# A transformer block with adaptive layer norm: row maxima split ahead of their transposition, V in 58 columns, two passes moved from VectorE to ScalarE

## The chip, the core and the metric

One core of a Trainium2 chip. It has TensorE (PE, with its weight loads PEld beside the matmuls), VectorE (DVE), ScalarE (ACT), GpSimd (POOL) and SyncE (SP), which here issues the DMAs. Each works through its own instructions in order; semaphores tie them together. The metric is the device time in microseconds, as the median of several runs.

## The reference

```python
mod = (_silu(c) @ w_mod).reshape(c.shape[0], 6, 1, -1)
sa, ca, ga, sb, cb, gb = (mod[:, 0], ..., mod[:, 5])
h = _layernorm(x, axis=-1) * (1 + ca) + sa
x = x + ga * _A_ref(h, A_wqkv, A_wo)      # attention, 16 heads of 28
h = _layernorm(x, axis=-1) * (1 + cb) + sb
x = x + gb * _B_ref(h, B_w1, B_b1, B_w2)  # dense 448 -> 1792, Mish, dense -> 448
...
scores = jnp.einsum("bhqd,bhkd->bhqk", q, k) * (Dh ** -0.5)
mask = (idx[:, None] - idx[None, :] >= 0) & (idx[:, None] - idx[None, :] < W)   # W = 256
scores = jnp.where(mask[None, None], scores, -1e9)
p = _softmax(scores, axis=-1)
o = jnp.einsum("bhqk,bhkd->bhqd", p, v)
```

2048 rows of 448 float32 numbers, one batch.

## The kernel before, in words

Nearly all matmuls run in fp32r, a float32 form that the matmul takes with fewer bits. An operand that needs more is split into a high part (rounded to fp32r by ACT or DVE) and a low part (the difference, by DVE or POOL), and the product is made as high x high + high x low + low x high. Names that end in h or hi and in l or lo are such parts: hh and hl of the normalised input, hho and hlo of the attention's output, Ph and Pl of the probabilities.

The 2048 rows are four groups of 512 (g = 0 to 3). Per group and head there is a slot (64 slots, s), and each slot has three units (192 units, u; k is the unit in the slot). In a unit, the main loop writes, in this order: the delayed stages that are due (pipe.step), the products of the low probabilities with V of three units ago (PV, tile pv), scores and mask for this unit (B, tile sB, then two exponentials P and Ph on ACT), the low part Pl = P - Ph of the last unit on POOL (SP, L768), a first pass over the scores of a slot three ahead for its row maxima (A: matmul sA, then a masked maximum on DVE into a column of mx, L713), in every sixth unit M2, and then fill. M2 serves a pair of slots: PE transposes their eight columns of maxima (tile mt, L719), DVE splits the result into two fp32r rows (mr, L721 and L722), and two DMAs put them into rows 84 and 85 of the query tiles, so that the score matmul subtracts the maximum. What the program writes first, an engine does first.

Fill is work of other groups: qkv products of the next group, then of the group just done the transposition of the attention output (gen_oT, tile ot, four chunks), the product with wo (gen_wo), and for the group after the next the transposed normalised input (gen_hT, tile tr, four chunks ci = 0 to 3). These are generators; each unit adds RATE[g] to a credit, and every piece drawn takes its cost from it:

```python
    RATE = {0: 0.56, 1: 0.87, 2: 0.87, 3: 0.65}
    def step(g):
        return next(fillers[g], 99.0) or RATE[g]
```

So a bare yield costs one unit. A second set of generators (side_step) hands out DVE and ACT work: the modulation's weighted sums (wm), layer norm (xin), weight splits. pipe.add(hold, f1, f2, ...) puts f1, f2, ... into the units that follow. The list later holds DMAs.

For a chunk of gen_hT, PE makes four transposes into a bank of PSUM tagged mm (of two). ACT writes hh from it (hT_hi, L257), a step later DVE makes the unrounded value in place (hT_y, L254) and subtracts hh from it into hl (L262). Then the bank is free. The attention output leaves pv as 60 rows per head (28 high, a row of ones for the sum and three of zeros, 28 low), two heads at partitions 0 and 64 of a tile o; four transposes (et) turn a pair, and ACT, DVE and POOL add the halves and divide (E2, E3).

After the attention (404 us), the MLP runs.

## Time and profile before

| | |
|---|---|
| median of 3 runs | 699.99 us (699.79 to 700.13) |
| the profiled execution | 699.71 us, span 698.0 us |
| granted TensorE clock | 1.000 |
| PE busy | 679.1 us, 97% of the span |
| DVE, ACT, POOL busy | 382.2, 391.7, 334.0 us |

The span runs from the first to the last instruction; the 1.7 us beside it lie around them. Busy time counts an engine's instructions without branches and waits. Since matmuls are pipelined, their records overlap, and an engine that is 97% busy may still lose a little between them.

### The profile page before, as it was taken

The numbers are of one execution on the slowest core, as the hardware profiler recorded it, in microseconds if no ns is written. First come the engines' busy times: TensorE is split into PE (matmuls) and PEld (weight loads), VectorE is DVE, ScalarE is ACT, GpSimd is POOL, SyncE is SP. The second block draws the span as 40 slices with busy tenths as digits, with TensorE's granted clock in tenths as the row PEclk, the third lists the DMA queues.
The fourth block names the chain that finished last, engine by engine and source line by source line (L and its number), as shares of the span: only waits on it lengthen the run. The fifth ranks groups of instructions, "written<-read, shape, count | busy, mean of one in ns | idle before, by whom it ended". The sixth has DMA issues, their size and how long they took to land.

```text
span 698.0 us, 11835 instructions
## 1 busy us (share of the span) xinstructions
PE 679.1 (97%) x3905; PEld 583.6 (84%) x3905; DVE 382.2 (55%) x1030; ACT 391.7 (56%) x741; POOL 334.0 (48%) x372
## 2 busy tenths in 40 slices
PE   8899999999999999999999899999999999999997
PEld 8777788888888888888887688888888888888886
DVE  5688657688665887655768754553125212521112
ACT  4638788777667867667878874353224222422221
POOL 7846779686766776666779967222010000000000
PEclk9999999999999999999999999999999999999999
DMA  7865665365662462763773165810250035001001
GB/s 213 263 226 198 217 213 176 119 201 164 179 206 85 156 211 89 191 211 108 226 217 112 53 211 173 212 29 4 103 120 1 2 105 121 0 2 53 0 1 53
DMA packets 75568, 91.13 MB, mean 131 GB/s; under 512 B 31632, under 2 KB 51838, under 8 KB 75508
## 3 DMA queue, kind: packets, MB, share of 16 engines
q1 hardware_dynamic: 75044, 90.38, 42.5%
q8 instruction: 31, 0.51, 0.3%
q14 instruction: 29, 0.24, 0.1%
q10 hardware_dynamic: 464, 0.00, 0.0%
HBM read 56.60 MB, written 32.51 MB: 128 GB/s over the span
## 4 chain that ended last, share of the span: by engine, by line
PE 82%; DVE 6%; DMA 4%; issue 2%; ACT 2%; POOL 1%; SPq 1%; POOLq 0%; DVEq 0%; ACTq 0%
PE z L950 21%; PE pv L778 9%; PE qk L315 7%; PE acc L1142 7%; PE acc L1140 6%; PE acc L1141 6%; PE sA L711 5%; PE wo L315 5%; PE sB L742 4%; PE qk_v L315 4%; DMA scr<-st 2%; DVE junk L713 2%; PE et L792 2%; PE warm L428 1%; PE sB L753 1%
## 5 line engine op out<-in xcount | busy, mean ns | idle before, releaser
L768 POOL TENSOR_TENSOR Pl<-P,Ph 128x512 fp32r<-128x512 f32 (+2 forms) x192 | 235.0, 1232 | 77.5 <-ACT Ph L761 44.9
L713 DVE CUSTOM_DVE_ANT_0 junk<-sA,mask 128x384 f32<-128x384 f32 (+2 forms) x256 | 135.0, 527 | 91.9 <-PE sA L711 84.5
L760 ACT ACTIVATE P<-sB 128x512 f32<-128x512 f32 (+2 forms) x192 | 109.6, 571 | 58.8 <-PE sB L757 33.7
L958 DVE TENSOR_TENSOR al<-t,ah 128x512 fp32r<-128x512 f32 x56 | 39.2, 699 | 188.6 <-ACT ah L957 188.6
L956 ACT ACTIVATE t<-z,b1c 128x512 f32<-128x512 f32 x56 | 38.4, 686 | 142.9 <-PE z L950 142.6
L761 ACT ACTIVATE Ph<-sB 128x512 fp32r<-128x512 f32 (+2 forms) x192 | 109.0, 568 | 0.0
L711 PE MATMUL sA<-k,q 84*128 84x384 f32 (+2 forms) x256 | 100.7, 396 | 2.6 <-DVE mx L713 1.8
L950 PE MATMUL z<-hlf,w 128*128 128x512 f32 x224 | 88.5, 395 | 0.0
L950 PE MATMUL z<-hhf,w 128*128 128x512 f32 x224 | 88.5, 395 | 0.0
L1140 PE MATMUL acc<-w2h,ah 128*128 128x448 f32 x224 | 82.0, 366 | 0.0
L1142 PE MATMUL acc<-w2h,al 128*128 128x448 f32 x224 | 81.9, 366 | 0.0
L1141 PE MATMUL acc<-w2l,ah 128*128 128x448 f32 x224 | 81.5, 364 | 0.0
L778 PE MATMUL pv<-Ph,v 128*60 128x256 f32 (+2 forms) x352 | 76.7, 292 | 0.6 <-ACT o L784 0.3
L778 PE MATMUL pv<-Pl,v 128*60 128x256 f32 (+2 forms) x352 | 73.8, 283 | 2.9 <-POOL Pl L768 2.0
L742 PE MATMUL sB<-q,k 128*128 128x256 f32 (+1 forms) x352 | 73.7, 283 | 0.6 <-DMA q<-mr 0.6
L950 PE MATMUL z<-hhf,w1l 128*128 128x512 f32 x168 | 66.3, 394 | 0.0
L742 PEld LDWEIGHTS sB<-q,k 128*128 128x128 f32 (+1 forms) x352 | 61.2, 188 | 2.0 <-DMA q<-mr 1.0
L778 PEld LDWEIGHTS pv<-Ph,v 128*60 128x60 f32 x352 | 45.7, 133 | 14.1 <-ACT o L784 1.9
L711 PEld LDWEIGHTS sA<-k,q 84*128 84x128 f32 x256 | 49.6, 195 | 8.0 <-DVE mx L713 5.3
L778 PEld LDWEIGHTS pv<-Pl,v 128*60 128x60 f32 x352 | 45.1, 132 | 11.9 <-POOL Pl L768 4.0
L950 PEld LDWEIGHTS z<-hlf,w 128*128 128x128 f32 x224 | 42.1, 188 | 10.1
L224 POOL COPY xn<-xn 128x64 f32<-128x64 f32 x12 | 4.5, 396 | 93.7 <-DVE xn L241 93.6
(167 smaller groups left out, 1305.0 us busy)
## 6 DMA issues: line engine op xcount, KB each, us to landing
scr<-st SPq DMA_DIRECT2D x24, 512.0 KB
k<-scr SPq DMA_DIRECT2D x48, 252.0 KB
q<-scr SPq DMA_DIRECT2D x64, 168.0 KB
scr<-st SPq DMA_DIRECT2D x32, 256.0 KB
x<-x1d SPq DMA_DIRECT2D x10, 448.0 KB
xin<-in_A_x_dram SPq DMA_DIRECT2D x8, 448.0 KB
xr<-in_A_x_dram SPq DMA_DIRECT2D x16, 224.0 KB
x1d<-xr SPq DMA_DIRECT2D x16, 224.0 KB
```

The costliest lines, as they stand in the source:

```text
L315: PE.matmul(p, b, a, start=(n == 0), stop=(n == 10))
L711: PE.matmul(p[:, c0:384], q[0:84, t * 128:(t + 1) * 128], k[0:84, t * 128 + c0:t * 128 + 384], start=True, stop=True)
L713: DVE.tensor_tensor_reduce(out=junk[:, c0:384], in0=p[:, c0:384], in1=mask[:, c0:384], scale=1.0, scalar=-3.0e38, op0=ALU.add, op1=ALU.max ...
L742: PE.matmul(p[:, c:c + 128 * (t1 - t0)], k[0:rows, jj * 128:(jj + 1) * 128], q[0:rows, t0 * 128:t1 * 128], start=(n == 0), stop=False, ski ...
L760: ACT.activation(P[:, c0:], p[:, c0:], AF.Exp, scale=SCALE)
L761: ACT.activation(Ph[u][:, c0:], p[:, c0:], AF.Exp, scale=SCALE)
L768: eng.tensor_tensor(Pl[u][:, a:b], Pt[u][:, a:b], Ph[u][:, a:b].bitcast(F32), op=ALU.subtract)
L778: PE.matmul(pv[0:60, t0 * 128:t1 * 128], V[j % NV][:, h, :], P[u][:, c:c + 128 * (t1 - t0)], start=(P is Ph and b == 0 and n == 0), stop=F ...
L950: PE.matmul(zb[n], ps[m][1], ps[m][0], start=(m == 0), stop=(m == 10))
L1140: PE.matmul(p, ah[n][:, ts], w2h[f], start=(f == 0), stop=False)
L1141: PE.matmul(p, ah[n][:, ts], w2l[f], start=False, stop=False)
L1142: PE.matmul(p, al[n][:, ts], w2h[f], start=False, stop=(f == NF - 1))
```

## The change

It has four parts.

1. A new M2a, written at the head of the unit that has M2 (ahead of pipe.step), splits the maxima before they are transposed: a cast of the 128x8 columns to fp32r and a subtraction, both from SBUF to SBUF on DVE, into ml, 128x16. M2 then makes one fp32r product of ml with an fp32r identity (ident1, cast once at the start), which gives 16 rows; DVE copies them with one cast, and the two DMAs read rows 0 to 7 and 8 to 15.
2. V has 58 columns a head instead of 60: one row of zeros instead of three. pv, o and et shrink to 58 and 122.
3. hT_two: for chunks 2 and 3 of groups 1 to 3, ACT makes the unrounded value in place right after hh; DVE keeps only the subtraction.
4. gen_oT: after the first chunk of groups 0 to 2 the piece costs 1.2 instead of one unit's rate, so the second chunk and the fill behind it are drawn later.

```diff
+    ident1 = kq.tile([128, 128], F32R, name="ident1")
+    DVE.tensor_copy(ident1, ident)
...
-    V = [(vp if j < 6 else vq).tile([128, H, 60], F32R, name=f"v{j}") for j in range(NV)]
+    V = [(vp if j < 6 else vq).tile([128, H, 58], F32R, name=f"v{j}") for j in range(NV)]
...
+    def hT_two(p, ci, hh):
+        hT_hi(p, ci, hh, 0)
+        if ci > 1:
+            ACT.activation(p, p, AF.Identity, scale=cols[:, 1, ci:ci + 1], bias=cols[:, 0, ci:ci + 1])
...
-            pipe.add(2, lambda p=p, ci=ci: hT_hi(p, ci, hh, 0), lambda p=p, ci=ci: hT_lo(p, ci, hh, hl, 0))
+            pipe.add(2, lambda p=p, ci=ci: hT_two(p, ci, hh), lambda p=p, ci=ci: hT_lo(p, ci, hh, hl, 0, ci < 2))
...
-            yield
+            yield 1.2 if ci == 0 and g < NG - 1 else None
             if g == NG - 1:
...
+    def M2a(pr):
+        ml[pr] = att.tile([128, 2, 8], F32R, name=f"ml{pr}", tag="ml", bufs=2)
+        m = mx[pr].rearrange("p a t -> p (a t)")
+        DVE.tensor_copy(ml[pr][:, 0], m)
+        DVE.tensor_tensor(ml[pr][:, 1], m, ml[pr][:, 0].bitcast(F32), op=ALU.subtract)
...
     def M2(pr):
         p = bank("tr", 1, f"mt{pr}")
-        PE.transpose(p[0:8, 0:128], mx[pr].rearrange("p a t -> p (a t)"), ident)
-        r = att.tile([8, 2, 128], F32R, name=f"mr{pr}", tag="mr", bufs=1)
-        DVE.tensor_copy(r[:, 0], p[0:8, 0:128])
-        DVE.tensor_tensor(r[:, 1], p[0:8, 0:128], r[:, 0].bitcast(F32), op=ALU.subtract)
+        PE.matmul(p[0:16, 0:128], ml[pr].rearrange("p i n -> p (i n)"), ident1, start=True, stop=True)
+        r = att.tile([16, 128], F32R, name=f"mr{pr}", tag="mr", bufs=1)
+        DVE.tensor_copy(r, p[0:16, 0:128])
...
-            PE.matmul(pv[0:60, t0 * 128:t1 * 128], V[j % NV][:, h, :], P[u][:, c:c + 128 * (t1 - t0)],
+            PE.matmul(pv[0:58, t0 * 128:t1 * 128], V[j % NV][:, h, :], P[u][:, c:c + 128 * (t1 - t0)],
...
-            PE.transpose(p[:, t * 128:t * 128 + 124], O2[pr % 2][0:124, t * 128:(t + 1) * 128], ident[0:124, 0:124])
+            PE.transpose(p[:, t * 128:t * 128 + 122], O2[pr % 2][0:122, t * 128:(t + 1) * 128], ident[0:122, 0:122])
...
+        turn = k == 0 and (a - 1) % 2 == 1 and LEAD <= a - 1 < NS
+        if turn:
+            M2a((a - 1) // 2)
         pipe.step()
...
-        if k == 0 and (a - 1) % 2 == 1 and LEAD <= a - 1 < NS:
+        if turn:
             M2((a - 1) // 2)
```

What stands in a row now. First VectorE around the transpose at 370.6 us (the unit with M2 for the 30th pair). Before, the maximum of sA_3, then that of the next pair's sA_0, then the two rows of mr:

```order
799 L713 ISA junk,mx_5426<-sA_3_5573,mask 128x384
800 L713 ISA mx_5426 128x1
801 L713 ISA junk,mx_5597<-sA_0_5598,mask 128x384
802 L713 ISA mx_5597 128x1
803 L721 CAST mr_5603<-mt_5601 8x128
804 L722 TENSOR_TENSOR mr_5603<-mt_5601,mr_5603 8x128
805 L198 TENSOR_TENSOR w1l<-w1p_5289,w_5226 128x448
```

After:

```order
822 L720 ISA junk,mx_5482<-sA_3_5628,mask 128x384
823 L720 ISA mx_5482 128x1
824 L727 CAST ml_5640<-mx_5482 128x8
825 L728 TENSOR_TENSOR ml_5640<-mx_5482,ml_5640 128x8
826 L720 ISA junk,mx_5656<-sA_0_5657,mask 128x384
827 L720 ISA mx_5656 128x1
828 L736 CAST mr_5662<-mt_5660 16x128
829 L200 TENSOR_TENSOR w1l<-w1p_5320,w_5282 128x448
```

The split has moved from behind mt to ahead of it, between the last maximum and mt.

Second, TensorE at the second chunk of the attention output of group 0 (140 to 142 us; sA_3 is the last score pass of the pair, mt its transpose). Before, one ot chunk ahead of pv and one behind mt:

```order
789 L711 MATMUL sA_3_2165<-k_3_148,q_1_460 128x384
790 L250 MATMUL ot_2168<-ident,on_996 128x128 x4
791 L778 MATMUL pv_2174<-Ph_2088,v_167 60x128
792 L778 MATMUL pv_2174<-Ph_2088,v_169 60x384
793 L778 MATMUL pv_2174<-Pl_2125,v_167 60x128
794 L778 MATMUL pv_2174<-Pl_2125,v_169 60x384
795 L742 MATMUL sB_2180<-q_0_377,k_1_144 128x384
796 L742 MATMUL sB_2180<-q_0_377,k_1_144 128x128
797 L753 LDWEIGHTS identr
798 L753 MATMUL sB_2180<-fdmask,identr 128x2x128
799 L711 MATMUL sA_0_2191<-k_4_150,q_2_461 128x384
800 L719 MATMUL mt_2194<-ident,mx_1999 8x128
```

After:

```order
789 L718 MATMUL sA_3_2187<-k_3_148,q_1_462 128x384
790 L792 MATMUL pv_2190<-Ph_2110,v_169 58x128
791 L792 MATMUL pv_2190<-Ph_2110,v_171 58x384
792 L792 MATMUL pv_2190<-Pl_2147,v_169 58x128
793 L792 MATMUL pv_2190<-Pl_2147,v_171 58x384
794 L756 MATMUL sB_2198<-q_0_379,k_1_144 128x384
795 L756 MATMUL sB_2198<-q_0_379,k_1_144 128x128
796 L767 LDWEIGHTS identr
797 L767 MATMUL sB_2198<-fdmask,identr 128x2x128
798 L718 MATMUL sA_0_2209<-k_4_150,q_2_463 128x384
799 L734 MATMUL mt_2212<-ident_156,ml_2193 16x128
800 L252 MATMUL ot_2218<-ident,on_1004 128x128 x4
```

The chunk that stood between sA_3 and mt now stands behind mt.

Third, ScalarE at chunks 2 and 3 of the normalised input of group 3 (269 to 272 us). Before:

```order
377 L257 ACTIVATE hh_3859<-tr_4078,cols 128x512
378 L760 ACTIVATE P_4094<-sB_4090 128x512
379 L761 ACTIVATE Ph_4095<-sB_4090 128x512
380 L797 ACTIVATE ol_4105<-et_4073 128x224
381 L257 ACTIVATE hh_3859<-tr_4107,cols 128x512
382 L760 ACTIVATE P_4123<-sB_4119 128x512
383 L761 ACTIVATE Ph_4124<-sB_4119 128x512
```

After:

```order
381 L259 ACTIVATE hh_3933<-tr_4122,cols 128x512
382 L292 ACTIVATE tr_4122<-tr_4122,cols 128x512
383 L774 ACTIVATE P_4139<-sB_4135 128x512
384 L775 ACTIVATE Ph_4140<-sB_4135 128x512
385 L811 ACTIVATE ol_4150<-et_4117 128x224
386 L259 ACTIVATE hh_3933<-tr_4152,cols 128x512
387 L292 ACTIVATE tr_4152<-tr_4152,cols 128x512
388 L774 ACTIVATE P_4168<-sB_4164 128x512
389 L775 ACTIVATE Ph_4169<-sB_4164 128x512
```

Each hh has the second pass right behind it, ahead of the next exponentials; DVE's L254 rows for these chunks are gone.

## The prediction

> **What bounds the kernel now.** I read the page first, then busy time by stage, then waits and instruction groups, and last the timeline around single transposes.

> ```profile
> span 698.0 us, 11835 instructions
> PE 679.1 (97%) x3905; PEld 583.6 (84%) x3905; DVE 382.2 (55%) x1030; ACT 391.7 (56%) x741; POOL 334.0 (48%) x372
> PE 82%; DVE 6%; DMA 4%; issue 2%; ACT 2%; POOL 1%; SPq 1%; POOLq 0%; DVEq 0%; ACTq 0%
> ...
> 40.00:140.00 100.00, 96.25 (x623) 78.86 (x622) 71.64 (x245) 73.43 (x163) 69.31 (x73) 1.00 0.59 190
> ...
> 340.00:404.00 64.00, 59.40 (x418) 50.26 (x416) 49.29 (x139) 54.22 (x108) 52.86 (x51) 1.00 0.47 140
> 404.00:698.00 294.00, 290.37 (x1355) 251.51 (x1352) 93.32 (x158) 98.91 (x156) 39.26 (x45) 1.00 0.25 71
> ```

> The stage rows give each engine's busy time in the order PE, weight load, DVE, ACT, POOL, then the clock (1.00 throughout). TensorE is the bound: whatever it waits for is added to the time, and work elsewhere costs only where PE waits for it. From 404 us on (the MLP) PE never rests and the change touches nothing. The attention stage, 40 to 404 us, is where it acts; there POOL is busy 69 to 83% of the time, which will matter. PE's waits are few:

> ```profile
> PE sA L711 <- DVE mx L713: 1.8, 4, 0.6
> PE qk L315 <- DVE hl L262: 1.7, 2, 0.9
> ...
> PE ot L250 <- DVE st L339: 1.0, 2, 0.5
> ...
> PE sB L742 <- DMA q<-mr: 0.6, 1, 0.6
> ```

> Columns: total us, times, longest.

> **What the change takes away.** The durations of the operations concerned, as count | busy us, mean ns | idle before (of mr's subtraction: shortest/median/longest):

> ```profile
> L742 PE MATMUL sB<-q,k 128*128 128x128 f32 x96 | 21.2, 221 | 0.0
> L792 PE MATMUL et<-ident,o 124*128 124x124 f32 x128 | 18.8, 268 | 0.0
> L719 PE MATMUL mt<-ident,mx 128*8 128x128 f32 x32 | 8.7, 273 | 1.6 <-DVE mx L713 1.6
> ...
> L722 DVE TENSOR_TENSOR mr<-mt,mr x32: 278/279/280, 44.1 to 391.5; 8x128 fp32r<-8x128 f32 x32
> ...
> L254 DVE TENSOR_SCALAR tr<-tr,cols 128x512 f32<-128x512 f32 x14 | 11.4, 812 | 0.7 <-ACT hh L257 0.7
> ...
> L457 ACT ACTIVATE tr<-tr,cols 128x512 f32<-128x512 f32 x2 | 1.5, 758 | 0.0
> ```

> 1. mt becomes an fp32r product of 128 columns. The nearest such row is sB's, 221 ns against 273 for the fp32 transpose: 32 x 52 = -1.7 us, all on PE, less the weight load, which lies beside the matmuls.
> 2. 58 rows of V. The streamed columns of pv stay the same, so those 704 matmuls gain nothing. The et transposes stream 122 columns for 124; 273 against 268 ns for 128 against 124 columns is 1.2 ns a column: 128 x 2.5 = -0.3 us. The two memsets are POOL work with cover.
> 3. ACT makes the second pass of chunks 2 and 3. DVE loses 6 x 812 ns, ACT gains 6 x 758. The waits of qk for hl show what that is worth:

> ```profile
> 270.37 0.81 DVE L254 TENSOR_SCALAR tr<-tr,cols 128x512 f32<-128x512 f32 x1
> ...
> 271.21 0.69 DVE L262 TENSOR_TENSOR hl<-tr,hh 128x512 fp32r<-128x512 f32 x1
> ...
> 272.05 0.47 PE L315 MATMUL qk<-hh,wq 128*128 128x512 f32 x1 [0.89 <-DVE hl L262]
> ```

> The bank of chunk 2 comes free when hl is done. Without the 0.81 us in front hl starts at once, and the wait of 0.89 goes; likewise its twin in the group before: -1.7 us. ACT's passes stand ahead of exponentials, but those wait for PE rather than the other way round (no row of PE's waits names P or Ph on ACT), so I price them at nothing.
> 4. The second ot chunk of groups 0 and 1 moves from ahead of a transpose to behind it:

> ```profile
> 140.09 0.66 PE L250 MATMUL ot<-ident,on 128*128 128x128 f32 x4 [0.49 <-DVE st L339]
> ...
> 141.02 0.08 DVE L713 DVE_READ_ACCUMULATOR2_ANT mx<- 128x1 f32 x1
> ...
> 141.58 0.27 PE L719 MATMUL mt<-ident,mx 128*8 128x128 f32 x1
> ```

> The wait of 0.49 us before ot goes and four matmuls of some 0.11 us leave the stretch, so PE comes to mt 0.9 us sooner, at 140.7. But DVE's queue to the last maximum (st, hlo, sA) is as long as before: the maximum is read at 141.10 as now. This gain is therefore not booked here; what becomes of it stands with mt, below. What comes late next is wo and xr, a unit behind; that unit's matmuls are their cover.
> 5. mr is one cast instead of cast and subtraction, so the DMA of row 85 starts 279 ns earlier: half of the 0.6 us wait of sB, -0.3.
> 6. The last transpose waits today behind the MLP's first chunk on DVE:

> ```profile
> 388.77 0.81 DVE L254 TENSOR_SCALAR trf<-trf,cols 128x512 f32<-128x512 f32 x1
> ...
> 390.70 0.08 DVE L713 DVE_READ_ACCUMULATOR2_ANT mx<- 128x1 f32 x1
> 390.84 0.27 PE L719 MATMUL mt<-ident,mx 128*8 128x128 f32 x1 [0.73 <-DVE mx L713]
> ```

> In the new order trf stands behind ml: -0.7.

> Together 1.7 + 0.3 + 1.7 + 0.3 + 0.7 = -4.7 us.

> **What it adds: a chain between the last maximum and mt.** Today mt can start as soon as the last maximum is read: 390.78 to 390.84, 0.06 us. Afterwards a cast and a subtraction stand between. Neither shape is in the trace. The nearest rows:

> ```profile
> L414 DVE TENSOR_SCALAR sT<-sT 112x4 f32<-112x4 f32 x1 | 0.1, 136 | 0.0
> L416 DVE TENSOR_TENSOR sT<-sT,cT 112x4 f32<-112x4 f32 x1 | 0.2, 164 | 0.0
> ```

> With 0.03 us between dependent DVE rows, the chain is 0.03 + 0.14 + 0.03 + 0.16 + 0.06 = 0.42 us. How much room is there? For one pair:

> ```profile
> 370.29 1.29 POOL L768 TENSOR_TENSOR Pl<-P,Ph 128x512 fp32r<-128x512 f32 x1 [0.26 <-PE pv L778]
> ...
> 370.39 0.08 DVE L713 DVE_READ_ACCUMULATOR2_ANT mx<- 128x1 f32 x1
> 370.62 0.27 PE L719 MATMUL mt<-ident,mx 128*8 128x128 f32 x1
> ```

> The maximum is read at 370.47, mt starts at 370.62: 0.15 us of room, 0.42 needed, so mt waits 0.27. I read these two rows for all 32 transposes (first mt 43.00, last 390.84); room runs from 0.06 to 1.18 us. In some pairs the new order also puts ahead of ml what stands behind the maximum on DVE today, at the first pair and at 337.2 for example

> ```profile
> 42.87 0.61 DVE L369 TENSOR_TENSOR v<-qk_v,v 128x448 fp32r<-128x448 f32 x1
> ...
> 43.40 0.50 DVE L241 TENSOR_SCALAR xin<-xin,mva,rsa 128x448 f32<-128x448 f32 x1
> ...
> 336.20 1.48 DVE L175 SCALAR_TENSOR_TENSOR wm<-wm,sT,wm 112x448 f32<-112x448 f32 x1
> ```

> The sum without any other hindrance: the first pair +1.4 (behind the v subtraction and a normalisation), the one at 337.2 +0.9 (behind a wm sum), those at 189.8 and 288.2 +0.6 each and 77.9 +0.5 (behind a wm product), 60.6, 347.7 and 370.6 +0.3 each, three more 0.2 together: 5.1. At 141.6 and its twin at 240.0, mt starts 0.42 after the maximum, about when it does today, but the ot chunk (0.44) now comes after it: +0.4 each. That makes +5.9 us. PE is in order: behind a late mt stand the next fill matmuls and pv.

> **POOL.** ml reads SBUF and writes SBUF; the removed subtraction read PSUM. In the trace this makes a difference:

> ```profile
> 78.83 1.05 DVE L175 SCALAR_TENSOR_TENSOR wm<-wm,sT,wm 112x448 f32<-112x448 f32 x1
> ...
> 152.84 1.29 POOL L768 TENSOR_TENSOR Pl<-P,Ph 128x512 fp32r<-128x512 f32 x1
> ...
> 152.92 1.46 DVE L241 TENSOR_SCALAR xin<-xin,mva,rsa 128x448 f32<-128x448 f32 x1
> ...
> L241 DVE TENSOR_SCALAR xin<-xin,mva,rsa x12: 499/611/1455, 41.1 to 251.3; 128x448 f32<-128x448 f32 x12
> ...
> 117.95 0.27 DVE L721 CAST mr<-mt 8x128 fp32r<-8x128 f32 x1
> ...
> 118.57 1.46 DVE L200 TENSOR_TENSOR wo<-wop,wo 64x448 fp32r<-64x448 f32 x1
> ...
> 403.15 1.02 DVE L768 TENSOR_TENSOR Pl<-P,Ph 128x256 fp32r<-128x256 f32 x1 [0.56 <-ACT Ph L761]
> ```

> A normalisation that starts while POOL subtracts ends 0.25 us after POOL does (1455 ns against 499 alone), and so does a subtraction of two SBUF tiles; mr, from PSUM, takes 278 to 280 ns whatever POOL does. Is an operation of 8 elements held likewise? The trace has none under Pl, so the price lies between the free 164 ns and the rest of a Pl, up to 1.3 us. I take the hold, because every operation on two SBUF tiles that starts with over 0.2 us of a Pl to go shows it, 11 of 11 from the wm sum at 78.83 to the last of the Pl on DVE at 403.15, at 256 and at 448 columns alike. At 370.6, Pl ends at 371.58, so ml ends near 371.60 and mt starts 1.04 late instead of 0.27. By the same reading: 60.6 and 347.7 +0.9 each, 165.6 and 264.0 +0.55 each, 189.8 and 288.2 +1.4, 337.2 +1.7, the others as above: +11.3 us. At five more (77.9, 141.6, 202.3, 240.0, 300.7) Pl and ml's subtraction start within 0.05 us of each other; where Pl is first, about 1.1 us is added, so all five make 16.8, the upper bound.

> [...]

> **Sum.** +11.3 - 4.7 = +6.6. A PE that stands longer at mt lets DVE catch up, so a third of the 1.8 us that sA waits for mx goes: -0.6. Net +6.0. The profiled execution took 699.71 us (span 698.0), so 705.7 for such a one; the median of the runs is 0.28 above it, 706.0.

> **Rivals.**
> - Short operations pass under POOL: +5.9 - 4.7 - 0.6 = +0.6, 700.6 us. For it: the hold was only seen from 256 columns up. Against: the 11 long ones.
> - The chain is hidden: DVE loses 32 x 279 ns and 6 x 812 ns, the maxima come earlier, the ot waits (1.0 us) go too, and only the two long queues (first pair, 337.2) still cost: 2.3 - 5.7 - 0.6 = -4.0, 696.0 us. Against: in the pairs with little room DVE is busy with xr and its statistics up to the last maximum, which the change leaves there. This one ends on the other side; it decides once the room has grown past 0.42 us in all but two pairs.
> - ACT's second passes delay exponentials: at 269.6 to 272.6 ACT has no gap, and if each of the six holds PE for its 758 ns, that is +4.5 on top of the first rival, 705.1. Against: ACT is 56% busy, and its exponentials wait for sB.

> **How the numbers follow.** A measurement here tells about 0.2% (1.4 us) from no change: faster is below 698.6, slower above 701.4. The hold 0.51 (slower 0.48, same 0.02, faster 0.01), short operations pass 0.26 (slower 0.03, same 0.16, faster 0.07), hidden 0.19 (faster), ACT 0.04 (slower). Faster 0.27, same 0.18, slower 0.55. The hold alone spans 700.3 (half of its 11.3) to 711.5 (16.8 for 11.3); the other cases reach down to 696.0. With a tenth cut at each end the range is 696.4 to 709.5.

> **What would show it.** Right: ml's subtraction lasts up to 1.3 us where Pl runs, ending with it; PE's waits for ml total about 10 us over some 15 transposes; the waits for hl, st and q<-mr are gone; mt takes 221 ns. Wrong: ml takes 140 to 170 ns throughout (first rival), or PE hardly waits for ml (second), or PE waits for P or Ph (third).

## The result, and the profile after

The changed kernel takes 720.56 us (median of 6 runs, 719.56 to 722.21) against 700.06 before (699.29 to 700.62): ratio 1.0292, 95% interval 1.0278 to 1.0305. The prediction was slower by 6.0 us, 706.0, with 709.5 as its upper end; the loss is 20.5 us. The profiled execution took 719.56 us, its span is 717.8 us; its granted clock is 0.992, that of the other five 0.987 to 0.993.

First the busy times and PE's waits in the profile after (total us, times, longest):

```profile
span 717.8 us, 11825 instructions
...
PE 683.9 (95%) x3905; PEld 586.7 (82%) x3905; DVE 396.1 (55%) x1057; ACT 396.5 (55%) x747; POOL 332.6 (46%) x372
...
PE mt L734 <- DVE ml L728: 17.4, 16, 2.8
PE pv L792 <- ACT o L798: 2.2, 5, 0.6
PE pv L792 <- POOL Pl L782: 2.1, 3, 1.3
PE sB L756 <- DMA scr<-st: 2.0, 1, 2.0
...
PEld sB L756 <- DMA q<-mr: 2.3, 1, 2.3
```

One row carries it: mt waits 17.4 us for ml, where it waited 1.6 for mx. The rows of qk for hl and of ot for st are gone, as forecast; pv's wait for o is new in this size. Before it was

```profile
PE pv L778 <- ACT o L784: 0.3, 1, 0.3
```

The one wait of sB is for the maxima's transfers: the row of the matmul names scr<-st, which landed at about the same time, but the weight load of the same product waits for q<-mr.

What ml itself took (shortest, median, longest ns):

```profile
L727 DVE CAST ml<-mx x32: 140/224/1231, 44.7 to 407.4; 128x8 fp32r<-128x8 f32 x32
L728 DVE TENSOR_TENSOR ml<-mx,ml x32: 166/168/1185, 44.9 to 408.6; 128x8 fp32r<-128x8 f32 x32
...
L734 PE MATMUL mt<-ident,ml x32: 223/233/279, 45.2 to 409.8; 128*16 128x128 f32 x32
```

The free durations are those of the estimate, 0.14 and 0.17 us. But both rows reach 1.2 us, the cast too. The timeline at the 30th and the 28th pair shows how:

```profile
386.18 1.27 POOL L782 TENSOR_TENSOR Pl<-P,Ph 128x512 fp32r<-128x512 f32 x1 [0.27 <-PE pv L792]
386.28 0.08 DVE L720 DVE_READ_ACCUMULATOR2_ANT mx<- 128x1 f32 x1
386.39 1.07 DVE L727 CAST ml<-mx 128x8 fp32r<-128x8 f32 x1
387.50 0.17 DVE L728 TENSOR_TENSOR ml<-mx,ml 128x8 fp32r<-128x8 f32 x1
...
387.72 0.23 PE L734 MATMUL mt<-ident,ml 128*16 128x128 f32 x1 [1.07 <-DVE ml L728]
```

```profile
359.27 3.73 POOL L782 TENSOR_TENSOR Pl<-P,Ph 128x512 fp32r<-128x512 f32 x3
359.69 0.88 DVE L727 CAST ml<-mx 128x8 fp32r<-128x8 f32 x1
360.61 1.18 DVE L728 TENSOR_TENSOR ml<-mx,ml 128x8 fp32r<-128x8 f32 x1
...
361.85 0.23 PE L734 MATMUL mt<-ident,ml 128*16 128x128 f32 x1 [1.94 <-DVE ml L728]
```

At 386.4 the cast starts 0.2 us into a Pl and ends with it, 387.46; the subtraction then runs free. At 359.7 three Pl stand back to back: the cast lasts to the end of the first, and by the time the subtraction starts, 0.04 us after the cast, POOL is in the next one, so the subtraction waits that out as well: 2 us for sixteen columns of arithmetic. Of the 32 pairs, 13 have a held cast (over 0.3 us), 9 a held subtraction, 4 both.

Then the granted clock. Busy time by stretch, the clock being the third number from the end:

```profile
65.00:67.00 2.00, 2.00 (x13) 1.70 (x11) 1.09 (x5) 2.00 (x5) 1.27 (x2) 0.53 0.02 4
67.00:69.00 2.00, 2.00 (x12) 1.67 (x11) 1.17 (x3) 1.42 (x3) 0.36 (x1) 0.61 0.67 195
...
360.00:362.00 2.00, 0.15 (x2) 0.16 (x3) 1.97 (x3) 1.20 (x3) 2.00 (x3) 1.00 0.96 295
362.00:364.00 2.00, 2.00 (x11) 1.69 (x10) 1.06 (x4) 0.00 (x0) 1.00 (x1) 0.52 0.14 46
364.00:366.00 2.00, 2.00 (x11) 1.76 (x11) 0.85 (x3) 1.09 (x2) 0.36 (x1) 0.62 0.20 30
```

PE works 0.15 us of the two before 362, and then runs at half clock until about 365.5. There are three such stretches, behind the waits at 64, 362 and 410 us. In them pv's products of 256 columns start every 0.21 us, elsewhere every 0.12 (medians); so each stretch, 3.4 us long, loses by estimate 2 x 0.48 + 2 x 0.38 = 1.7 us. In the profile before, the clock was 1.00 throughout.

So the account on the profiled executions (+19.85): waits at mt +15.8, half clock +5.1, waits for o +1.9, for the maxima's way to sB +1.4; off again 1.7 (hl), 1.0 (st), 32 x 0.04 = 1.3 (mt's own), which makes +20.2. With sA's waits for mx, 0.7 us shorter (1.8 to 1.1), it is 19.5.

### The profile page after: what moved, and what is told of

It reads as the page before. It is cut to its first block, busy times and chain, and to the rows that moved or that the text cites. A ratio compares the mean times of both kernels' runs of the same rounds, so it can differ in the third digit from the quotient of the medians.

```text
span 717.8 us, 11825 instructions
## 1 busy us (share of the span) xinstructions
PE 683.9 (95%) x3905; PEld 586.7 (82%) x3905; DVE 396.1 (55%) x1057; ACT 396.5 (55%) x747; POOL 332.6 (46%) x372
## 4 chain that ended last, share of the span: by engine, by line
PE 81%; DVE 10%; ACT 4%; DMA 2%; issue 2%; SPq 1%; POOL 0%; DVEq 0%; ACTq 0%; POOLq 0%
PE z L964 20%; PE pv L792 9%; PE qk L322 7%; PE acc L1160 6%; PE acc L1158 6%; PE acc L1159 6%; PE sA L718 5%; PE sB L756 4%; PE wo L322 4%; PE qk_v L322 4%; DVE junk L720 3%; DMA scr<-st 2%; PE et L806 2%; DVE ml L727 1%; DVE ml L728 1%
## 5 line engine op out<-in xcount | busy, mean ns | idle before, releaser
L792 PE MATMUL pv<-Ph,v 128*58 128x256 f32 (+2 forms) x352 | 77.9, 296 | 2.5 <-ACT o L798 2.2
L792 PE MATMUL pv<-Pl,v 128*58 128x256 f32 (+2 forms) x352 | 74.6, 286 | 2.3 <-POOL Pl L782 2.1
L792 PEld LDWEIGHTS pv<-Ph,v 128*58 128x58 f32 x352 | 45.5, 133 | 17.8 <-ACT o L798 5.1
L792 PEld LDWEIGHTS pv<-Pl,v 128*58 128x58 f32 x352 | 45.3, 132 | 11.1 <-POOL Pl L782 3.5
L964 PEld LDWEIGHTS z<-hhf,w 128*128 128x128 f32 x224 | 42.1, 188 | 8.2
```

The source lines that it names most:

```text
L792: PE.matmul(pv[0:58, t0 * 128:t1 * 128], V[j % NV][:, h, :], P[u][:, c:c + 128 * (t1 - t0)], start=(P is Ph and b == 0 and n == 0), stop=F ...
L964: PE.matmul(zb[n], ps[m][1], ps[m][0], start=(m == 0), stop=(m == 10))
```

## The experiments

Theory H: POOL's Pl holds ml's operations, and PE waits at mt. R1: the chain is too long by itself. R2: the moved fill and ScalarE's passes make a good part of the loss.

**The split alone, and everything but the split.** `p1_only` is the kernel before with part 1 of the diff; `p234` the changed kernel with the old M2:

```diff
# p234
+        PE.transpose(p[0:8, 0:128], mx[pr].rearrange("p a t -> p (a t)"), ident)
...
-            M2a((a - 1) // 2)
```

> The kernel before with only the maxima's split ahead of their transposition (M2a, ml, fp32r mt). Theory H (POOL's Pl holds ml's cast and subtraction, and mt waits for ml): nearly the whole loss is here, 716 to 722 us, with 17 us or more of PE's waits at mt. Rival R2 (the moved fill and ScalarE's extra passes make a good part of the loss, by PE's new waits for o, Pl and the DMA of q): 712 us or less.

> The changed kernel with the old M2: V in 58 columns, ScalarE's passes, the later ot chunk. Theory H: 695 to 699 us, since the waits of qk for hl (1.7) and of ot for st (1.0) and the 0.3 of et go. Rival R2: 703 us or more.

p1_only: 729.70 us, ratio 1.0425 (1.0393 to 1.0457). p234: 698.85, ratio 0.9980 (0.9965 to 0.9995). The whole loss is the split's, and R2 falls. That the split alone costs 29 us, more than with the other parts, was not expected by either: mt waits longer there,

```profile
PE mt L729 <- DVE ml L723: 27.3, 20, 2.8
```

because how much of a Pl is left when ml starts hangs on where the fill puts the maximum. With the other parts the fill comes later and VectorE has less to do, and the waits at mt happen to be ten us shorter: two pairs that pay 2.5 us each here (200.5 and 305.9 us) pay nothing in the changed kernel.

**No Pl on POOL.** In both kernels SP, the step in which POOL makes Pl, is left out, and the second product reads Ph again:

```diff
-        if 0 <= u - 1 < NU:
-            SP(u - 1)
...
-            PE.matmul(pv[...], V[j % NV][:, h, :], P[u][:, c:c + 128 * (t1 - t0)],
+            PE.matmul(pv[...], V[j % NV][:, h, :], Ph[u][:, c:c + 128 * (t1 - t0)],
```

> The kernel before without POOL's subtractions Pl; the second product with V uses Ph again, so PE's work is the same. Left out: the low part of the probabilities. Baseline for the next run: 696 to 700 us, since PE's waits for Pl (2.7 us) go.

> The changed kernel without POOL's subtractions Pl, likewise. Theory H: ml's cast takes 140 to 175 ns and its subtraction 165 to 170 ns everywhere, PE's waits at mt fall from 17.4 to under 6 us, no stretch at half clock, and the time is within -4 to +3 us of the kernel before without Pl. Rival R1 (the chain itself, not POOL, is what is too long): mt's waits stay above 12 us and the time is 12 us or more above it.

Before without Pl: 695.01, ratio 0.9942 (0.9920 to 0.9965). After without Pl: 696.44, ratio 0.9947 (0.9928 to 0.9965). The 20.5 us between the two kernels shrink to 1.4. ml's rows there, in the tile's answer, and mt's wait:

```profile
L727 DVE CAST ml<-mx x32: 138/171/351, 44.2 to 386.4; 128x8 fp32r<-128x8 f32 x32
L728 DVE TENSOR_TENSOR ml<-mx,ml x32: 166/168/1055, 44.4 to 386.7; 128x8 fp32r<-128x8 f32 x32
...
  PE mt L734: 4.4, 8
```

H holds and R1 falls: the same chain in the same order costs 4.4 us of waits when POOL makes no Pl. Not "everywhere" as expected, but nearly: the cast of 351 ns and the subtraction of 1055 are one pair's and ran beside another subtraction on POOL (wop).

**The half clock.** Ahead of three late mt stand nine or ten bf16 matmuls into mt's own bank:

```diff
         p = bank("tr", 1, f"mt{pr}")
+        for _ in range({2: 9, 27: 10, 31: 10}.get(pr, 0)):
+            PE.matmul(p[:, 0:384], identr, fdmask[:, 0:384], start=True, stop=True)
```

> The changed kernel with nine or ten bf16 matmuls of 384 columns into mt's own bank ahead of three of the late mt (the pairs at 64.0, 361.9 and 409.8 us), so that PE works through most of the wait. Theory C (the half clock after these waits is caused by the idle time, and costs 1.7 us each): no half clock behind them and 3 to 5 us less than the changed kernel, 715.5 to 717.5. Rival: the dips don't hang on the idle time, or the added matmuls cost as much as they save: 719 to 722 us.

717.44 us, ratio 1.0242 (1.0205 to 1.0280), 3.1 us less than the changed kernel for 29 matmuls more; the two intervals just overlap. Behind the pair at 359 us:

```profile
358.00:360.00 2.00, 1.68 (x12) 0.84 (x10) 1.97 (x3) 1.25 (x3) 2.00 (x3) 1.00 0.83 290
360.00:362.00 2.00, 2.00 (x14) 1.83 (x14) 1.48 (x5) 0.48 (x1) 1.08 (x1) 1.00 0.03 12
```

The clock stays at 1.00, and so at the other two places. But two stretches at half clock stand elsewhere: one at 45.8 us, behind the first pair's wait of 1.7 us, which had none in the changed kernel, and one at 15.0 us, ahead of the attention, where PE's records show no gap (16 matmuls of one column each fill 2 us there). So three stretches became two, 1.7 us less; sB's waits fell from 2.0 to 0.7; the price of a stretch doesn't follow from the 3.1 us.

Which waits are hit is not a matter of length alone: the longest one, 2.8 us at 349.7, was not, those of 1.6 to 1.9 at 64, 362 and 410 were. The traces show what else counts. In every one of them the stretches begin a whole number of 3.413 us apart (87 and 14 times in the changed kernel, from 65.13 to 362.09 and 409.88). Cut into windows on this grid, the changed kernel shows, PE's busy time first behind the comma:

```profile
61.72:65.13 3.41, 1.81 (x17) 1.45 (x15) 3.23 (x10) 3.07 (x8) 1.85 (x2) 1.00 0.76 286
65.13:68.54 3.41, 3.41 (x17) 2.97 (x16) 1.82 (x8) 3.29 (x7) 1.14 (x2) 0.50 0.29 78
345.02:348.44 3.42, 1.93 (x13) 1.41 (x11) 3.14 (x4) 2.91 (x6) 3.36 (x5) 1.00 0.85 308
348.44:351.85 3.41, 2.14 (x14) 1.63 (x15) 2.51 (x7) 0.73 (x2) 1.20 (x1) 1.00 0.01 4
358.68:362.09 3.41, 1.47 (x10) 1.11 (x11) 3.34 (x6) 2.52 (x5) 3.34 (x4) 1.00 0.95 271
362.09:365.50 3.41, 3.41 (x13) 2.92 (x13) 1.53 (x6) 1.08 (x2) 0.91 (x1) 0.50 0.08 24
```

The wait of 2.8 us is cut in two by the edge at 348.44, so each window keeps 1.9 to 2.1 us of work, and no half clock follows; the wait of 1.9 us lies almost whole in one window. Over the 2846 windows of the fourteen traces, counted from PE's records, half clock follows every one of the 15 with PE busy for at most 43%, 7 of the 16 from 44 to 53%, and above that none but the one at 15.0 us. So theory C's cause, idle time of PE, is shown for these traces, in the form that it falls into one window; the share between 44 and 53% doesn't decide, and what does is open. By the same count the experiment alone would not have shown it: without the added matmuls its three windows had PE busy for 46 to 52%.

**A later mt.** M2 is written one unit after M2a:

```diff
-        if turn:
+        if k == 1 and (a - 1) % 2 == 1 and LEAD <= a - 1 < NS:
             M2((a - 1) // 2)
```

> The changed kernel with M2 (the fp32r product mt, mr, its DMAs) written one unit later, at k = 1; the split M2a stays where it is. Theory H: only the wait at mt is harmful, so with a whole unit (3.5 us) between ml and mt it goes: PE's waits at mt under 1 us, no stretch at half clock, 695 to 698 us, under the kernel without the split (698.85). Rival R3 (VectorE held by POOL harms others too, and the maxima then reach the queries late): waits of sB for q<-mr or of other users of VectorE take the place, 700 us or more.

> The same kernel as late, for its profile. Theory R3: waits of sB for q<-mr (the maxima come a unit later to the queries, and units of the first group last 2 us only) make the 23 us, most of them before 140 us; mt itself hardly waits. Rival: waits for o, Pl or other work on VectorE, spread over all groups.

722.72 us, ratio 1.0314 (1.0287 to 1.0342); the profile is that of a repeat, 723.56:

```profile
PE sB L756 <- DMA q<-mr: 13.9, 20, 1.4
PE mt L734 <- DVE ml L728: 3.2, 4, 1.7
PE sA L718 <- DMA k<-scr: 3.0, 4, 1.0
```

The wait at mt falls from 17.4 to 3.2 us (not under 1, as theory H had it), and the wait for the maxima's DMA takes its place, 20 times and in all groups: R3 in its mechanism, but not "most of them before 140 us" (6 of the 20). The way from maximum to sB has too little slack for either. Of the 23.8 us more of span, PE's idle time is 17.1 and one stretch at half clock 1.7; the other 5.0 lie within PE's busy time and are not explained.

**ScalarE's passes alone, and the later ot chunk alone.**

> The kernel before with only ScalarE's second passes for chunks 2 and 3. The prediction's step 3: the two waits of qk for hl go, 698.0 to 698.8 us. Rival (the passes delay o and the exponentials): PE waits for o on ScalarE instead, 699.5 us or more.

> The kernel before with only the later ot chunk. The prediction left its 1.0 us out, since mt would take it; with the old mt, which needs no split, the wait of ot for st (1.0) goes and the kernel gains up to 1 us: 699.0 to 700.0. Rival (the moved chunk puts o or hho late on ScalarE): 700.5 or more, with new waits of pv for o at 140 and 238 us.

p3_only (part 3 of the diff on the kernel before): 699.46, ratio 0.9989 (0.9969 to 1.0009). p4_only (part 4): 699.96, ratio 0.9989 (0.9972 to 1.0005). The first lies between the theory's range and the rival's, the second in the theory's; neither is told from no change. Their waits say why. In p3_only the wait of qk for hl is gone, and pv waits 1.2 us for o on ScalarE (0.3 before), the engine that got the passes. In p4_only the wait of ot for st is gone, and

```profile
PE pv L778 <- POOL Pl L768: 3.1, 5, 1.3
PE pv L778 <- ACT o L784: 2.1, 5, 0.6
```

stand in its place (2.0 and 0.3 before): the rival's waits, at the rival's place. The five waits for o in the changed kernel (0.3, 0.5, 0.6, 0.4 and 0.3 us, the second and third at 147 and 247, behind the moved ot chunks) are these five, and not the one of 0.9 at 64.6 us that p3_only has.

**Without any split.** Only numerator and sum must use the same shift, so the maximum need not be exact. `hi` is p234 with mx written as fp32r by the maximum itself, mt an fp32r product of 8 columns, one DMA into row 84; row 85 stays zero, and sB reads 85 rows in group 0.

```diff
-            mx[i // 2] = att.tile([128, 2, 4], F32, name=f"mx{i}", tag="mx", bufs=2)
+            mx[i // 2] = att.tile([128, 2, 4], F32R, name=f"mx{i}", tag="mx", bufs=2)
...
-        PE.transpose(p[0:8, 0:128], mx[pr].rearrange("p a t -> p (a t)"), ident)
+        PE.matmul(p[0:8, 0:128], mx[pr].rearrange("p a t -> p (a t)"), ident1, start=True, stop=True)
...
-            dma(t[86:128].bitcast(F32), p[86:128].bitcast(F32))
+            dma(t[85:128].bitcast(F32), p[85:128].bitcast(F32))
```

> The kernel of p234 with the maxima written as fp32r by the masked maximum itself and no split at all: mt is one fp32r product of 8 columns, mr one cast, one DMA into row 84 (row 85 of the queries stays zero; the shift only has to be the same for numerator and sum). Theory H: nothing stands between maximum and mt, so it gains mt's 1.7 us and half the cast's time over p234 without the loss: 695.5 to 698 us. Rival: the same as p234, 698.5 to 700 us, since PE's other waits take it up.

711.39 us, ratio 1.0151 (1.0124 to 1.0179): a miss for both. sB waited 9.7 us for q<-mr, four times, all before 126 us. `hi2` sends row 84 in two DMAs again, `hi3` also takes the copies of the constant rows back to row 86 and zeroes row 85 by a memset:

```diff
# hi3
+    POOL.memset(Q2[0][64:86].bitcast(F32), 0.0)
...
+    for t in Q2[1:-1]:
+        POOL.memset(t[64:86].bitcast(F32), 0.0)
...
-            dma(t[85:128].bitcast(F32), p[85:128].bitcast(F32))
+            dma(t[86:128].bitcast(F32), p[86:128].bitcast(F32))
```

> As hi (maxima straight in fp32r, no split, row 85 zero), but with two DMAs a pair again, one for each slot's half of row 84, so that the eight DMA semaphores are dealt out in the order of the kernel before. Theory D (hi lost because its single DMA shifted that order, and sB then waited for a semaphore that a slow transfer shares): PE's 9.7 us of waits of sB for q<-mr fall under 1.5 us and the time is 695.5 to 698 us. Rival (the single transfer itself was slow, or the maxima come late for another reason): 705 us or more.

> As hi2, but the copies of the constant rows start at row 86 again, as in the kernel before (42 rows instead of 43), and row 85 of two query tiles is set to zero by a memset instead. Theory K (the copies of 43 rows are slow, and sB's waits put down to q<-mr are for them, since all four lie before 140 us, where these copies run): the waits fall under 1.5 us, and the time is 695.5 to 698 us, under both kernels. Rival (the maxima's own DMAs come late): 710 us or more as for hi2.

hi2: 715.11, ratio 1.0209 (1.0188 to 1.0230), and

```profile
PE sB L747 <- DMA q<-mr: 11.5, 4, 4.3
```

Theory D falls. hi3: 696.79, ratio 0.9943 (0.9925 to 0.9961), with no row of sB and q<-mr left: theory K. hi3 took back sB's row count in group 0 too (86 for 85), but the kept traces part the two by their semaphore events. In hi2 each of the seven copies of 43 rows has two events, the second 8.3 to 10.9 us after the issue; in hi3 each of the seven of 42 rows has fifteen, the last after 3.2 to 5.0 us. And each of the four waits of sB ends with the last of the five events of a transfer q<-mr: the one issued at 61.38 us has four by 63.04 and the fifth at 67.87, and sB starts at 67.91. So it was the transfers, late behind the copies of 43 rows, and not the matmul; why a copy of 43 rows has two events and one of 42 fifteen was not shown.

hi3 is faster than both kernels, and than p234 (0.9980) by 2.1 us in the medians: with nothing ahead of it, the fp32r transposition takes 229 ns instead of 273, and VectorE has one operation less. Which of the two the gain comes from was not parted.

> hi3 without the later ot chunk. Theory P (the later chunk pushes the last group's fill together, so that pv waits 1.7 us for Pl at 377 and half a clock stretch follows): that wait falls under 0.9 us, no stretch at half clock near 380, and about 1 to 3 us less than hi3, 694 to 696, though the two waits of ot for st (1.0 us) come back. Rival (the chunk's move is worth its 1.0 us): 697.5 us or more.

hi3 without part 4: 696.84, ratio 0.9951 (0.9934 to 0.9968). What theory P said of the waits comes: pv's for Pl fall from 3.3 to 2.1 (none over 0.6), the stretch at half clock that hi3 has at 378 us is gone, and the waits of ot for st (1.0) are back. But the time doesn't: the two versions are the same to 0.1 us, though pv's waits for o fall from 3.4 to 1.3 too. The later chunk gains nothing.

## Why the prediction was wrong

- **What bounds it**, and where it would be lost: right. PE waits at mt, behind ml, where POOL runs Pl.
- **The hold on short operations**: right, and shown by the runs without Pl: PE's waits at mt fall from 17.4 to 4.4 us. The subtraction at 8 columns takes 166 ns free and up to 1185 held.
- **The size of the hold: this step failed.** The prediction priced the cast at 0.14 us everywhere and let only the subtraction be held, once: +11.3 us, and -0.7 at the last pair. The cast is held as well (up to 1231 ns). Measured: 17.4 us of waits at mt, +15.8 over before. A held cast with a free subtraction behind it costs no more than the held subtraction that was forecast (at 370.6, now 387.7: 1.04 forecast, 1.07 measured). But after a held cast the next Pl can be running, and then both are held: +2.8 at 337.2 (now 349.7; 1.7 forecast), +1.9 at 347.7 (now 361.9; 0.9 forecast), and +1.0 at 390.8 (now 409.8), where step 6 had -0.7.
- **Where Pl stands** was wrong at other pairs, and that is chance as much as reading, since parts 2 to 4 move the fill: three that were given at most 0.2 cost 2.7 us together (136.8, 237.0 and 375.5), the two at 189.8 and 288.2, given 1.4 each, cost nothing. At 141.6 and 240.0 (+0.4 each, or 1.1 more if Pl is first) Pl was first, 1.2 us of wait each. The first pair (+1.4) came to 1.7 of wait, 1.3 more than before.
- **The row that was misread.** The normalisation that the prediction quoted as held, 1455 ns, has only one SBUF tile as input (beside two columns of scalars), like the cast; all six of xin that start with over 0.2 us of a Pl to go are longer than when free (0.71 to 1.46 us, 0.50 free). It was read as a case of the subtraction.
- **The clock: a term that was missing.** 5.1 us, behind three waits; to two of them the prediction added 0.9 us each, the third it had as gone. It said the clock is 1.00 throughout and took that as given, though the waits it added were among the longest of the kernel.
- **Step 1** (mt -1.7): mt takes 233 ns, not 221: -1.3. **Step 2** (et -0.3): about right in p234, 267 ns against 268 (-0.2); the mean of 271 in the changed kernel has the half clock in it, its median is 267.
- **Step 3** (-1.7): the wait went. Alone, the part costs pv a wait for o on ScalarE and is worth 0.6 us, with an interval that takes in no change; there the rival that ScalarE delays others was right in kind, but it named the exponentials and P, and it is o. In the changed kernel that wait doesn't appear. **Step 4**, left out of the sum for mt's sake: the wait of ot (1.0) goes and waits for o (+1.9) come; alone it is worth nothing. All of parts 2 to 4 give 1.4 us.
- **Step 5** (-0.3): turned round. The second transfer of that pair is issued 1.3 us after mt starts (1.5 before), as meant, but lands 5.6 us after its issue (4.0 before), and one sB waits 2.0 us for it (0.6 before). What slowed it is open. **Step 6** (-0.7): without Pl on POOL the last mt doesn't wait at all; with it the hold takes its place, 1.7 us.
- **sA's waits** (-0.6): 1.8 to 1.1, as forecast.
- **The other two rivals** fell: ml is not short under POOL, and the chain is not hidden.

## What to carry to other kernels

Ahead of an operation for which the busiest engine waits, a cast or a subtraction of two tiles that reads and writes SBUF on VectorE is a risk where GpSimd is as busy as here (68% of the time from 40 to 414 us): its length became the rest of GpSimd's subtraction, up to 1231 ns for a cast of 140 and up to 1185 for a subtraction of 166, and two such operations in a row paid twice, 2.1 us at 359.7. The old split of the transposed row, which read PSUM, was not held (272 to 280 ns for each of its two operations, beside a Pl or not). Price a wait of some 2 us on TensorE not only by its length but by the clock behind it: three waits of 1.6 to 1.9 us had 3.41 us at half clock behind them, one of 2.8 us had none, and which it was hung on where the wait fell in the windows. And when a step can be dropped altogether (here the exactness of a shift that cancels), drop it before making it faster.
